# A searched list schedule against a written fixed order per engine: two attention and two feed-forward layers on one core

## The chip, the cores and the metric

One core of one Trainium2 chip. The metric is the device time of one execution in microseconds (us), the median over several executions. Each execution also has a mean granted TensorE clock, as a share of full speed.

## The reference, cut to what matters

Two pairs of layers with the same weights, on x of 2048 x 512: linear attention with 32 heads of 16, then a ReGLU feed-forward of 1376 columns.

```python
def _A_ref(x, wqkv, w_phi, wo):
    ...
    phi_k = concatenate([softmax(pk), softmax(-pk)], -1)      # phi_q likewise
    kv  = einsum("bhsf,bhsd->bhfd", phi_k, v)                 # over ALL 2048 rows
    z   = einsum("bhsf->bhf", phi_k)
    num = einsum("bhqf,bhfd->bhqd", phi_q, kv)
    den = einsum("bhqf,bhf->bhq", phi_q, z)[..., None] + 1e-6
    return (num / den).transpose(...).reshape(B, S, D) @ wo
def _B_ref(x, W_gate, W_up, W_down):
    gate = relu(x @ W_gate); return (gate * (x @ W_up)) @ W_down
x = A_x
x = x + _A_ref(_layernorm(x), ...);  x = x + _B_ref(_layernorm(x), ...)
x = x + _A_ref(_layernorm(x), ...);  x = x + _B_ref(_layernorm(x), ...)
```

`kv` is a sum over all rows, so no row's numerator can start before the last row's K and V are done. Each attention layer thus holds a serial passage, and the feed-forward layers are long stretches of independent matmuls.

## The kernel before: the parts that matter

The kernel lists 3748 operations, each with its engine, its reads and writes, a duration and a name. Dependencies follow from reads and writes. A list scheduler then decides which operation stands where on each engine; 20 seeded perturbations, found by a search, are applied in a row.

```python
WINDOW = {"sp": 24, "act": 64, "pe": 400, "dve": 40, "pool": 24}

    def schedule(self):
        self.setup_search()
        best = self.first_order()          # list scheduling, forward and backward passes
        for seed in self.STEPS:            # 20 seeded perturbations of the priorities
            best = self.step(best, seed)
        _, start, finish, _ = best
        ...
        self.order = sorted(self.ops, key=lambda o: (o.start, o.idx))
        return self.order
```

From the order, `prepare` plans the fewest semaphore waits; each engine runs its list in sequence. Three groups of operations are named in the argument below:

```python
    def knorm(self, t, tag):               # K normalisation, one tile of 128 rows
        op("dve", ... tensor_reduce ..., f"{tag} Zk {t}")
        op("dve", ... reciprocal ..., f"{tag} rZk {t}")
        parts = [("pool", 0, 2)] if t < NT - 2 else [("pool", 0, 1), ("dve", 1, 2)]
        ...                                # GpSimd: expk *= 1/Zk           "phik"
    def kv_acc(self, t, tag):              # 8 matmuls of 65 columns        "kvacc"
        ...  [r("phik", t, bank), r("v", t), r("vones")], [self.RP[bank]] ...   # banks 0 and 1
    def q_proj(self, st, ring, tag, ...):  # groups of 4 matmuls of 512     "q st c"
        ...  banks = [next(ring) for _ in range(w)] ...
    def num(self, t, nring, wring, tag):   # 8 matmuls of 144 columns       "num"
        ...  [r("expq", st, c, s), r("kvbd", s, 0), r("kvbd", s, 1), ...] ...
```

Between the last "kvacc" and the first "num", VectorE writes the accumulated sums as block matrices ("kvbd"). The "q" groups have no part in that and can stand there as filler.

The softmax here doesn't subtract the row's maximum and nothing guards it: scores larger than these inputs give would overflow.

Of the kernel before, what the change touches and what calls it, by code (L numbers as in the profile page):

```python
# [10 lines left out]
ALL_STREAMS = ENG_NAMES + DMA_QUEUES  # L11

# [38 lines left out]
class Program:  # L51
# [9 lines left out]
    WEIGHTS = (5.0, 10.0, 20.0, 30.0)  # L61
    PASSES = 12
    STEPS = (
        540311766, 892937877, 494555537, 744661157, 897750461, 867948165, 881829396, 760774381, 571941922, 293543564,
        578814794, 296541888, 687658138, 1028335485, 543616021, 388973925, 782538568, 34231468, 301009185, 271859956,
    )

    def __init__(self, nc, window, n_dma_sems=48):
        self.nc = nc
        self.ops = []  # L70
        self.window = window
        self.n_dma_sems = n_dma_sems
# [54 lines left out]
    def setup_search(self):  # L127
        self._derive_deps()
        ops = self.ops
        n = len(ops)  # L130
        self.succ = [[] for _ in range(n)]
        for o in ops:
            for d in o.deps:
                self.succ[d].append((o.idx, True))
            for d in o.order_deps:
                self.succ[d].append((o.idx, False))
        rank = [0.0] * n
        for o in reversed(ops):
            lat = o.lat if o.lat is not None else self.DMA_START + o.dma_bytes / self.DMA_BW + self.DMA_TAIL
            rank[o.idx] = max([rank[q] + (lat + self.TO[ops[q].eng] if d else o.occ) for q, d in self.succ[o.idx]], default=lat)  # L140
        self.rank = rank

    def first_order(self):
        best = None
        for weight in self.WEIGHTS:
            prio = [weight * o.idx - self.rank[o.idx] - o.boost for o in self.ops]
            for _ in range(self.PASSES):
                span, start, finish = self._forward(prio)
                if best is None or span < best[0]:
                    best = (span, start, finish, prio)  # L150
                prio = [t - o.boost for t, o in zip(self._backward(start, finish), self.ops)]
        return best

    def step(self, best, seed):
        ops = self.ops
        span, start, finish, prio = best
        rng = random.Random(seed)
        kind = seed % 4
        a = rng.uniform(0.0, span)
        w = (6e3, 15e3, 40e3, span)[int(rng.random() * 4)]  # L160
        amp = (150.0, 500.0, 1500.0, 4000.0)[int(rng.random() * 4)]
        share = (0.02, 0.1, 0.4, 1.0)[int(rng.random() * 4)]
        base = prio if kind < 2 else [s - o.boost for s, o in zip(start, ops)] if kind == 2 else [t - o.boost for t, o in zip(self._backward(start, finish), ops)]
        new = []
        for o in ops:
            x, y = rng.random(), rng.random()
            p = base[o.idx]
            if a - w / 2 <= start[o.idx] <= a + w / 2 and x < share:
                p += (2 * y - 1) * amp
            new.append(p)  # L170
        span, start, finish = self._forward(new)
        return span, start, finish, new

    def schedule(self):
        self.setup_search()
        best = self.first_order()
        for seed in self.STEPS:
            best = self.step(best, seed)
        _, start, finish, _ = best
        self.makespan = max(finish)  # L180
        for o in self.ops:
            o.start, o.finish = start[o.idx], finish[o.idx]
        self.order = sorted(self.ops, key=lambda o: (o.start, o.idx))
        return self.order

    def _forward(self, prio):
        ops, succ, TO = self.ops, self.succ, self.TO
        n = len(ops)
        npred = [len(o.deps) + len(o.order_deps) for o in ops]
        ready = [0.0] * n  # L190
        avail = {e: {} for e in ENG_NAMES}
        pending = {e: [o.idx for o in ops if o.eng == e] for e in ENG_NAMES}
        place = [0] * n
        for e in ENG_NAMES:
            for j, i in enumerate(pending[e]):
                place[i] = j
        done = [False] * n
        free = {e: 0.0 for e in ENG_NAMES}
        q_free = 0.0
        pool_end = dve_end = 0.0  # L200
        first = {e: 0 for e in ENG_NAMES}
        for o in ops:
            if npred[o.idx] == 0:
                avail[o.eng][o.idx] = 0.0
        start, finish = [0.0] * n, [0.0] * n
        nxt = {e: None for e in ENG_NAMES}
        dirty = set(ENG_NAMES)
        inf = float("inf")
        for _ in range(n):
            for e in dirty:  # L210
                lst = pending[e]
                f = first[e]
                while f < len(lst) and done[lst[f]]:
                    f += 1
                first[e] = f
                lim = f + self.window[e]
                fe = free[e]
                if e == "pool":
                    fe = max(fe, dve_end - self.PORT_POOL)
                bt, bp, bi = inf, inf, -1  # L220
                for i, t in avail[e].items():
                    if place[i] >= lim:
                        continue
                    if t < fe:
                        t = fe
                    if e == "dve":
                        pt = ops[i].port
                        if pt is not None and t < pool_end - pt:
                            t = pool_end - pt
                    if t < bt or (t == bt and (prio[i] < bp or (prio[i] == bp and i < bi))):  # L230
                        bt, bp, bi = t, prio[i], i
                nxt[e] = (bt, bp, bi) if bi >= 0 else None
            dirty = set()
            st, _, i = min(k for k in nxt.values() if k is not None)
            o = ops[i]
            e = o.eng
            start[i] = st
            free[e] = st + o.occ
            if o.lat is None:
                q_free = max(st + self.DMA_START, q_free) + o.dma_bytes / self.DMA_BW  # L240
                fin = q_free + self.DMA_TAIL
            else:
                fin = st + o.lat
            finish[i] = fin
            if e == "pool":
                pool_end = fin
                dirty.add("dve")
            elif e == "dve" and o.port is not None:
                dve_end = fin
                dirty.add("pool")  # L250
            done[i] = True
            del avail[e][i]
            dirty.add(e)
            for q, is_data in succ[i]:
                eq = ops[q].eng
                npred[q] -= 1
                if is_data:
                    t = fin + TO[eq]
                    if t > ready[q]:
                        ready[q] = t  # L260
                if npred[q] == 0:
                    avail[eq][q] = ready[q]
                    dirty.add(eq)
        return max(finish), start, finish

    def _backward(self, start, finish):
        ops, succ, TO = self.ops, self.succ, self.TO
        n = len(ops)
        T = max(finish)
        nsucc = [len(x) for x in succ]  # L270
        late = [T] * n
        avail = {e: set() for e in ENG_NAMES}
        free = {e: T for e in ENG_NAMES}
        for o in ops:
            if nsucc[o.idx] == 0:
                avail[o.eng].add(o.idx)
        out = [0.0] * n
        nxt = {e: None for e in ENG_NAMES}
        dirty = set(ENG_NAMES)
        for _ in range(n):  # L280
            for e in dirty:
                nxt[e] = min([(-min(late[i] - (finish[i] - start[i]) + ops[i].occ, free[e]), -finish[i], i) for i in avail[e]], default=None)
            dirty = set()
            k, _, i = min(x for x in nxt.values() if x is not None)
            o = ops[i]
            out[i] = free[o.eng] = -k - o.occ
            avail[o.eng].remove(i)
            dirty.add(o.eng)
            for d in o.deps + o.order_deps:
                e = ops[d].eng  # L290
                nsucc[d] -= 1
                late[d] = min(late[d], out[i] - TO[o.eng] if d in o.dset else out[i] + (finish[d] - start[d]) - ops[d].occ)
                if nsucc[d] == 0:
                    avail[e].add(d)
                    dirty.add(e)
# [735 lines left out]
```

## Time and profile before

| | before |
|---|---|
| median of 4 runs beside the changed kernel | 394.75 us (393.81 to 395.34) |
| profiled span, mean clock | 391.6 us, 0.999 |
| TensorE work at its full rate | 363.1 us |
| first matmul starts | 3.21 us |
| last K/V accumulation of layer 0 | 54.18 us |
| first numerator matmul of layer 0 | 56.76 us |
| last K/V accumulation of layer 2 | 238.99 us |
| last matmul starts | 388.25 us |

The third row is the sum over all 2379 matmuls of the start-to-start time of each shape, as the prediction works it out. In the trace of this kernel, neighbouring matmuls of one shape start 216 ns apart at 512 columns (median; between 82 and 236 us also where two groups alternate), 109 at 256, 82 at 192, 63 at 144 and 32 at 65; at 128 columns it is mostly 107 in the first 12 us and 56 from 18.9 us on. The times below it are starts of matmuls, found by laying the trace beside the program's order. Together they give a measure, called the **loss** of a stretch: time between the first and the last start in it, less the full-rate work of the matmuls that start there. The lines of the profile itself are shown in the prediction.

### The profile page before, as it was taken

What the parts mean: (1) busy time and instruction counts of PE and PEld (TensorE: products, weight loads), DVE (VectorE), ACT (ScalarE), POOL (GpSimd) and SP (SyncE); (2) the same over time, 40 slices, a digit from 0 to 9 for tenths busy, and PEclk for the clock granted to TensorE, in tenths of its full rate; (3) what the DMA queues carried; (4) which work ended last, traced back from release to release, by engine and by line L of the source; (5) the groups of instructions that cost most, each with busy time, mean ns of one, the idle gap of its engine ahead of it and who ended that gap; (6) DMA issues with size and microseconds to landing.
All of it is one profiled execution on the core that took longest, in us unless ns stands there. A gap on an engine that the chain in (4) does not pass through costs nothing.

```text
span 391.6 us, 6419 instructions
## 1 busy us (share of the span) xinstructions
PE 369.0 (94%) x2336; PEld 201.8 (52%) x2379; DVE 268.1 (68%) x551; ACT 201.5 (51%) x381; POOL 170.2 (43%) x287
## 2 busy tenths in 40 slices
PE   5898988999999999999999997979999999999996
PEld 4444444576744554454444464456774445454443
DVE  5989878887766889766675776978875676322222
ACT  5787869742643413534354475965652561443340
POOL 7597952771543383533433652466544252000000
PEclk9999999999999999999999999999999999999999
DMA  6752492332221225301110120233233123100001
GB/s 195 195 80 57 114 364 53 70 65 47 54 51 29 41 54 83 68 2 27 27 15 0 27 28 2 41 62 68 62 69 79 27 43 83 41 13 15 27 28 55
DMA packets 66080, 24.08 MB, mean 61 GB/s; under 512 B 57888, under 2 KB 65024, under 8 KB 66048
## 3 DMA queue, kind: packets, MB, share of 16 engines
q1 hardware_dynamic: 65328, 23.07, 26.3%
q10 hardware_dynamic: 720, 0.59, 0.5%
q8 instruction: 19, 0.31, 0.4%
q14 instruction: 13, 0.11, 0.1%
HBM read 7.91 MB, written 2.10 MB: 26 GB/s over the span
## 4 chain that ended last, share of the span: by engine, by line
PE 84%; DMA 5%; DVE 4%; ACT 3%; issue 2%; POOL 1%; SPq 0%; POOLq 0%; DVEq 0%
PE ps L795 34%; PE ps L844 19%; PE ps L654 9%; PE ps L774 6%; PE ps L727 5%; PE ps L685 3%; PE ps L743 3%; PE ps L821 2%; DMA oT<-osb 2%; PE ps L699 2%; DMA yT<-ytile 1%; ACT expq L730 1%; DMA x_sb<-in_A_x_dram 1%; DVE tsc L763 1%; ACT expk L688 0%
## 5 line engine op out<-in xcount | busy, mean ns | idle before, releaser
L795 PE MATMUL ps<-yT,Wgu 128*128 128x512 bf16 (+1 forms) x789 | 173.8, 336 | 0.5
L795 PEld LDWEIGHTS ps<-yT,Wgu 128*128 128x128 bf16 x800 | 75.7, 98 | 62.0 <-ACT expk L803 1.4
L844 PE MATMUL ps<-Wd,hT 128*128 128x512 bf16 (+2 forms) x356 | 103.5, 373 | 0.4
L797 ACT ACTIVATE gate_sb<-ps 128x512 bf16<-128x512 f32 (+1 forms) x100 | 50.4, 513 | 82.7 <-PE ps L795 71.8
L673 POOL TENSOR_TENSOR expk<-expk,rZk 128x1024 bf16<-128x1024 bf16 (+1 forms) x32 | 59.6, 1876 | 33.1 <-DVE rZk L668 27.6
L844 PEld LDWEIGHTS ps<-Wd,hT 128*128 128x128 bf16 (+1 forms) x363 | 35.2, 98 | 35.8
L805 DVE TENSOR_TENSOR hT<-gate_sb,expk 128x512 bf16<-128x512 bf16 (+1 forms) x65 | 26.8, 422 | 29.4 <-ACT expk L803 23.4
L588 DVE BATCH_NORM_STATS2 stats<-x_sb 128x6 f32<-128x512 bf16 x64 | 42.6, 680 | 4.8 <-DMA x_sb<-in_A_x_dram 4.2
L401 ACT ACTIVATE numbf<-ps 128x432 bf16<-128x432 f32 x64 | 33.0, 539 | 20.1 <-PE ps L743 19.5
L666 DVE TENSOR_REDUCE Zk<-expk 128x64 f32<-128x1024 bf16 x32 | 38.1, 1205 | 4.5 <-ACT expk L688 2.6
L846 DVE TENSOR_TENSOR x_sb<-x_sb,ps 128x512 bf16<-128x512 bf16 (+1 forms) x33 | 22.0, 670 | 26.8 <-PE ps L844 26.6
L768 POOL TENSOR_TENSOR osb<-tsc 128x512 bf16<-128x512 bf16 x28 | 32.3, 1155 | 17.6 <-DVE tsc L763 17.6
L774 PE MATMUL ps<-wo_p,oT 128*128 128x512 bf16 x117 | 35.3, 379 | 3.9 <-DMA oT<-osb 3.5
L727 PE MATMUL ps<-yT,Wqp 128*128 128x512 bf16 x123 | 34.6, 379 | 2.3 <-ACT expq L730 2.1
L730 ACT ACTIVATE expq<-ps 128x1024 bf16<-128x1024 f32 (+1 forms) x40 | 32.2, 861 | 7.2 <-PE ps L727 5.9
L743 PE MATMUL ps<-kvbd,expq 128*128 128x144 bf16 x256 | 33.6, 226 | 2.4 <-DVE kvbd L716 2.1
L595 POOL TENSOR_SCALAR rv<-mv 128x1 f32<-128x1 f32 (+1 forms) x53 | 12.6, 240 | 53.6 <-DVE mv L590 53.1
L803 ACT ACTIVATE expk<-ps 128x512 bf16<-128x512 f32 (+1 forms) x65 | 32.2, 501 | 6.3 <-PE ps L795 6.2
L596 POOL TENSOR_TENSOR rstd<-rv,mhalf 128x1 f32<-128x1 f32 (+1 forms) x53 | 31.5, 597 | 3.0
L631 DVE TENSOR_SCALAR ytile<-x_sb,mv,rstd 128x512 bf16<-128x512 bf16 x52 | 22.1, 426 | 12.4 <-POOL rstd L596 11.7
L754 POOL TENSOR_TENSOR zm<-numbf 128x64 f32<-128x64 bf16 x28 | 10.5, 375 | 45.8 <-DVE numbf L401 33.0
L657 ACT ACTIVATE expk<-ps 128x512 bf16<-128x512 f32 x44 | 23.7, 603 | 12.5 <-PE ps L654 12.0
(78 smaller groups left out, 428.9 us busy)
## 6 DMA issues: line engine op xcount, KB each, us to landing
out_dram<-x_sb SPq DMA_DIRECT2D x15, 128.0 KB, 1.7
x_sb<-in_A_x_dram SPq DMA_DIRECT2D x3, 512.0 KB, 6.4
Wgu<-in_B_W_gate_dram SPq DMA_DIRECT2D x4, 344.0 KB, 4.0
Wgu<-in_B_W_up_dram SPq DMA_DIRECT2D x4, 344.0 KB, 5.9
Wd<-in_B_W_down_dram SPq DMA_DIRECT2D x5, 256.0 KB, 7.7
yT<-ytile SPq DMA_TRANSPOSE x60, 2.5
hT<-in_A_wqkv_dram ACTq DMA_DIRECT2D x4, 128.0 KB, 3.0
x_sb<-in_A_x_dram SPq DMA_DIRECT2D x4, 128.0 KB, 3.5
```

The source lines that it names most:

```text
L401: return e.activation(out, in_, ACT.Copy) if hasattr(e, "activation") else e.tensor_copy(out, in_)
L588: op("dve", (lambda t: lambda e: e.bn_stats(k.stats6[:, t, :], k.x_sb[:, t, :]))(t), [r("x", t)], [r("st", t)], 685, f"{tag} stats {t}")
L654: op("pe", (lambda ic, bank, W: lambda e: e.matmul(k.pb[bank][:], k.yT[:, ic, t * 128:(t + 1) * 128], W[:, ic, :], start=(ic == 0), stop=( ...
L666: op("dve", lambda e: e.tensor_reduce(k.Zk[:, zb, :], k.expk[:, t, :, :, :].rearrange("p g s (h f) -> p (g s h) f", f=16), AX.X, ALU.add), ...
L673: op(eng, (lambda kv, u0, n: lambda e: e.tensor_tensor(kv, kv, k.rZk[:, rb, u0 * 32:u0 * 32 + n].unsqueeze(2).to_broadcast([P, n, 16]), AL ...
L727: op("pe", (lambda c, ic, bank: lambda e: e.matmul(k.pb[bank][:], k.Wqp[:, ic, c * 128:(c + 1) * 128], k.yT[:, ic, st * 512:(st + 1) * 512 ...
L730: op("act", (lambda c0, s, b0: lambda e: e.activation(k.expq[:, st, c0:c0 + w, s, :], k.ps[:, b0:b0 + w, :], ACT.Exp, scale=(1.0 - 2.0 * s ...
L743: op("pe", (lambda s, c, j, g0, bank: lambda e: e.matmul(k.pb[bank][:, j * GW:(j + 1) * GW], k.expq[:, st, c, s, tt * 128:(tt + 1) * 128], ...
L774: op("pe", (lambda c, bank: lambda e: e.matmul(k.pb[bank][:], k.oT[:, ob, c, :], k.wo_p[:, c, :], start=(c == 0), stop=(c == NC - 1)))(c, ...
L795: op("pe", (lambda bank, W, ic, fc, Mf: lambda e: e.matmul(k.pb[bank][0:Mf, 0:n], W[:, ic, fc * 128:fc * 128 + Mf], k.yT[:, ic, c0:c0 + n] ...
L797: op("act", (lambda Mf, gb, gs: lambda e: e.activation(k.gate_sb[0:Mf, gs, 0:n], k.pb[gb][0:Mf, 0:n], ACT.Relu))(Mf, gb, gs), [self.RP[gb] ...
L844: op("pe", (lambda fc, Kf, u, c0, bank, m0, m1: lambda e: e.matmul(k.pb[bank][:, m0:m1], k.hT[0:Kf, u, c0:c0 + 128], k.Wd[0:Kf, fc, m0:m1] ...
```

## The change

The scheduler goes. A written table gives, for each engine, the sequence of operation numbers in base 36; `schedule` only simulates that order to get start times for planning the waits. The order is said to have been annealed (improved by random moves) against an in-order simulation with drawn DMA delays and noise on durations; the code doesn't show how it was found. Matmuls of one accumulation group nearly always stay together. The operations and their dependencies are the same.

```diff
+ORDER = {
+    "act": ("6 7 9 8 15 1a 10 24 1p 1k 2o 1u 2e 3t 3u 2y 3d 3v 4h 4f 4g 3j 5l 5n 5m 68 69 ..."),
+    "dve": ("1v 1w v 25 26 1z 2f 2g 29 2p 1f 2q 2j 33 35 2z 31 30 34 32 36 2t 4u 4t 4w 4v ..."),
+    "pool": ("p 2 n 0 3 1 4 j 1x 1y q 27 28 m 2h 2i 2r 2s 37 38 3c k 39 l 3f o 3i 4x 4y 4z ..."),
+    "pe": ("r s t u 11 12 13 14 w x y z 16 17 18 19 1b 1c 1d 1e 20 21 22 23 1l 1m 1n 1o ..."),
+    "sp": ("a 5 b c d e g f h i 3e 3b 3h 3k 56 58 5c 5a 8p 8n 8t 8r 9a 9f 8v 8x 97 94 8z ..."),
+}
...
     def schedule(self):
-        self.setup_search()
-        best = self.first_order()
-        for seed in self.STEPS:
-            best = self.step(best, seed)
-        ...
+        self._derive_deps()
+        seq = {e: [int(x, 36) for x in ORDER[e].split()] for e in ENG_NAMES}
+        assert sorted(i for s in seq.values() for i in s) == list(range(len(ops)))
+        ...                       # start times by stepping through seq in order
         return self.order
-    def _forward(self, prio): ...
-    def _backward(self, start, finish): ...
```

(Tables and functions are cut.) As a static check I wrote the old order as such a table: the program that comes out is the old one, waits included. So the order is all that differs.

## The prediction

> **What bounds the kernel now.** I read the page's busy rows first, then a table of engine time by stretch, then the waits, then the timelines of TensorE, GpSimd and VectorE where the table shows holes.
>
> ```profile
> span 391.6 us, 6419 instructions
> PE 369.0 (94%) x2336; PEld 201.8 (52%) x2379; DVE 268.1 (68%) x551; ACT 201.5 (51%) x381; POOL 170.2 (43%) x287
> ```
>
> TensorE is the bound: 94% busy, nobody else above 68%. There are 2379 weight loads, one for each matmul, but 2336 matmul rows, so 43 matmul records are missing and small "gaps" of a whole matmul are not gaps. The same by stretch (columns: stretch, then busy time and count for PE, weight loads, DVE, ACT, POOL, then clock, DMA share, GB/s):
>
> ```profile
> 0.00:13.00 13.00, 7.75 (x52) 5.38 (x54) 7.83 (x21) 7.49 (x13) 7.35 (x25) 1.00 0.73 233
> 13.00:57.00 44.00, 39.30 (x296) 20.20 (x300) 39.49 (x59) 35.04 (x52) 36.37 (x38) 1.00 0.55 140
> 57.00:82.00 25.00, 22.79 (x172) 13.98 (x172) 20.59 (x53) 19.60 (x36) 12.76 (x28) 1.00 0.37 86
> 82.00:236.00 154.00, 152.64 (x914) 81.18 (x932) 112.91 (x221) 65.14 (x131) 70.32 (x108) 1.00 0.21 37
> 236.00:262.00 26.00, 20.72 (x169) 11.95 (x169) 18.60 (x47) 19.40 (x29) 10.02 (x20) 1.00 0.20 37
> 262.00:388.00 126.00, 125.25 (x741) 68.94 (x753) 67.85 (x154) 54.79 (x122) 33.37 (x70) 1.00 0.20 47
> ```
>
> Idle TensorE time is stretch minus busy: 5.3 in the opening, 4.7 in the first K/V stage, 2.2 where the first attention goes over into the feed-forward part, 1.4 in 154 us of full work, 5.3 at the second such passage, 0.8 in the next 126 us, and 3.6 after 388 (last residual and store). So two passages and the opening hold nearly all of it; 280 us of the span are full, and no order can shorten them. What TensorE waits for (total, times, longest):
>
> ```profile
> PE ps L774 <- DMA oT<-osb: 3.5, 3, 2.7
> PE ps L546 <- DMA hT<-in_A_wqkv_dram: 3.2, 1, 3.2
> PE ps L685 <- DMA yT<-ytile: 2.2, 2, 1.3
> PE ps L727 <- ACT expq L730: 2.1, 2, 1.1
> PE ps L743 <- DVE kvbd L716: 2.1, 2, 1.6
> ```
>
> The 3.2 is the first load and stays. The others are links of two serial chains: K normalisation up to the accumulated K·V, and from there num, normalise, transpose by DMA, output projection, layer norm, transpose by DMA, first gate matmul. In the K/V stage GpSimd is a second bound (timeline of POOL):
>
> ```profile
> 14.37 0.23 POOL L595 TENSOR_SCALAR rv<-mv 128x4 f32<-128x4 f32 x1 [4.39 <-DVE mv L590]
> 33.99 3.86 POOL L673 TENSOR_TENSOR expk<-expk,rZk 128x1024 bf16<-128x1024 bf16 x2 [0.76 <-DVE rZk L668]
> 39.70 14.32 POOL L673 TENSOR_TENSOR expk<-expk,rZk 128x1024 bf16<-128x1024 bf16 x8 [1.84 <-DVE ytile L629]
> ```
>
> From 14.37 to 39.70 + 14.32 = 54.0 it works all but 0.76 + 1.84 = 2.6 us, and the first layer's last accumulation can only follow it.
>
> [...]from 147.84 us on, 24 recorded gate/up matmuls of 512 columns take 5.56 us; less the last one's 0.379 that is 5.18 between first and last start, 225 ns over 23 steps, or 216 over 24, as one record is missing there. That gives the floor: 1333 matmuls of 512 columns x 0.2157 + 342 of 256 x 0.109 + 128 of 192 x 0.0825 + 256 of 144 x 0.0625 + 256 of 65 x 0.032 + 64 of 128 x 0.056 = 363 us (shapes from the groups by form, counts completed from the program). The span stands 391.6 - 363 = 28.6 above it. [...]201.8 us of weight loads lie beside 152.64 busy in 154. So interleaving two groups, as the old order does, costs TensorE nothing by itself, and running groups whole saves nothing by itself.
>
> **The change part by part.** The instruction order tool shows the same 3748 operations with the same dependencies; only the order on each engine, and the waits that follow from it, differ. Nothing is removed or added, so busy times per engine stay (369, 268, 201, 170), and the gain must come out of 28.6 us. Of these, 3.2 (first load), 3.6 (tail: both orders end on the last tile's 22 half-width down matmuls, then residual and store) and about 2 (the first 48 narrow matmuls run at some 0.1 us apart against 0.057 later) are fixed. About 20 us can be moved.
>
> On TensorE, runs of equal instructions fall from 887 to 346: groups of 4 (11 for down) stay together. A group that shared TensorE with another finishes up to 4 x 0.2157 = 0.86 us earlier when it runs alone, so its evacuation starts earlier, while the second ends when it did. In the full stretches that is slack; on the chains it is worth something.
>
> *First passage, to 82 us.* Before, VectorE puts the first K reduction (1.18) ahead of the last layer-norm aggregate, so GpSimd starts its block at 14.37. After, the aggregates of tiles 4 to 7 come first: about 1.4 earlier (1.18 and the 0.2 of an aggregate that stood behind it). GpSimd then finishes the statistics of tiles 8 to 11 before its first two K products (3.82 together) and not after; their normalised rows, transposes and K matmuls come up to 4 us earlier, which should remove most of the 2.2 us wait for yT and part of the 2.6 us idle on GpSimd. Its work is fixed at 39.65 - 2.6 = 37 us, so it ends at best near 14.37 - 1.4 + 37 = 50, against 54.0; I take half of the idle as removed: 54.0 - 1.4 - 1.3 = 51.3, so 2.7. The new order has then done 6 query matmuls (1.3 us) less, which serve as filler in the chain behind. There the old order lost 2.2 and the new one puts output projections 0 and 1 right behind each other some 7 us after the first num, where the old one needed 64.68 - 56.76 = 7.9: some wait stays. Net 0.5. Together 3.2.
>
> *Second passage, 236 to 262.* Rows of the TensorE timeline:
>
> ```profile
> 241.01 0.42 PE L743 MATMUL ps<-kvbd,expq 128*128 128x144 bf16 x4 [1.61 <-DVE kvbd L716]
> 241.89 0.30 PE L743 MATMUL ps<-kvbd,expq 128*128 128x144 bf16 x2 [0.45 <-DVE kvbd L716]
> 250.76 1.04 PE L774 MATMUL ps<-wo_p,oT 128*128 128x512 bf16 x4 [0.43 <-DMA oT<-osb]
> 259.94 0.81 PE L774 MATMUL ps<-wo_p,oT 128*128 128x512 bf16 x3 [2.68 <-DMA oT<-osb]
> ```
>
> The new order leaves one query group (0.86) between the last accumulation and num where the old one left one matmul (0.2): 2.1 falls to about 1.4. Output projection 0 then stands 5 x 0.86 + 28 x 0.0625 = 6.1 after the first num; the chain needs about 7.3 (old 249.15 - 241.01 = 8.1, less 0.6 as num now runs whole, rounded for waits), so 1.2 is lost. Projection 3 has a first gate group and more queries ahead of it: of its 2.68 I keep 0.3, and 0.9 for the transposed rows of tile 1. Sum 3.8 against 5.8 idle in the old order with the small ones: 2.0 gained.
>
> *Full stretches.* 2.2 us of idle together. A fixed order tried against drawn delays may save some and whole groups may lose some: 0.3 gained. *Tail:* 0.
>
> Sum 3.2 + 2.0 + 0.3 = 5.5, so 395.0 - 5.5 = **389.5**.
>
> **The rivals.** *The order does what it was made for:* an annealed order takes most of the movable 20 us, say 9: 386. For it: it was judged under delays, and the old one was a greedy list with 20 perturbations. Against it: GpSimd's 37 us of work and the two DMA transposes of 2.4 us in each passage are serial whatever the order. *New waits take their place:* with coarser groups TensorE has fewer points at which to slip filler in; one late transpose (the longest landing was 4.5 us against 2.4) stops everything behind it. 154 us at 99% busy would drop to 98%: +1.5 there and +1 in the other full stretch, gains in the passages as above or half: 390 to 395. *The chains decide and nothing moves:* the passages are bound by VectorE and ScalarE (18.6 and 19.4 busy of 26): 393 to 395. Three weight loads (344, 344 and 256 KB) now stand between output transposes 1 and 2 on the same queue; at 343 GB/s, the rate of the stretch from 50 to 60 us, their 0.94 MB cost 2.8 us if a transpose gets behind them.
>
> **Range and chances.** 5.5 is a sum of two passages each unsure by some 2 us, and full stretches by 1.5: about 3.2 together, 4 at 80%, wider on the fast side for the first rival. Range 384.5 to 394. Faster by 2% means under 387.2, 2.3 below my middle: 0.27. Slower by 2% needs 8 us of new waits in a kernel that is full for 280 us: 0.04. Within 2%: 0.69.
>
> **What would show it.** Right: busy sums unchanged; idle TensorE in the first 82 us from 12.2 to about 9, at the second passage from 5.3 to about 3.5, elsewhere within 1 us of 2.2; GpSimd's last K product of the first layer near 51; the longest wait for oT below 1.5. Wrong: idle over 4 us in the full stretches (second rival), GpSimd's block ending at 54 again (third), or both passages under half of their idle time (first). A wait for weights of the feed-forward part would be a miss of mine altogether.

## The result, and the profile after

The changed kernel takes **389.93 us** (median of 4 runs, 388.86 to 391.21) against 394.75 us (4 runs, 393.81 to 395.34): ratio **0.988**, 95% interval 0.984 to 0.992. A ratio is the mean time of one kernel's fast runs over that of the other's of the same rounds, so not quite the ratio of the medians quoted.

The head of the page of the changed kernel, to be laid beside the first lines of the prediction:

```profile
span 389.5 us, 6419 instructions
PE 373.7 (96%) x2379; PEld 203.0 (52%) x2379; DVE 264.8 (68%) x551; ACT 202.3 (52%) x381; POOL 168.5 (43%) x287
```

The busy time of TensorE rose from 369.0 to 373.7 while the kernel got shorter. Its work has not grown: this trace has all 2379 matmul records, the one before lacked 43, and this one holds a stretch at half clock (below). Of the 4.7 us some 2.9 are the missing records, as rows laid into the holes give, and 1.7 the half clock. By stretch (columns: stretch; busy time and count of PE, weight loads, DVE, ACT, POOL; clock, DMA share, GB/s):

```profile
0.00:13.00 13.00, 7.22 (x51) 4.92 (x52) 8.28 (x23) 6.15 (x11) 7.70 (x24) 1.00 0.70 219
13.00:57.00 44.00, 41.16 (x313) 21.04 (x312) 39.02 (x62) 37.55 (x57) 35.88 (x40) 0.98 0.54 137
57.00:82.00 25.00, 24.05 (x176) 15.13 (x175) 19.24 (x48) 19.23 (x35) 12.92 (x29) 0.97 0.37 92
82.00:236.00 154.00, 154.00 (x942) 81.05 (x941) 114.81 (x222) 64.67 (x130) 70.30 (x108) 1.00 0.20 38
236.00:262.00 26.00, 23.66 (x181) 13.81 (x180) 19.70 (x51) 21.15 (x36) 11.55 (x25) 1.00 0.20 40
262.00:388.00 126.00, 123.64 (x727) 67.02 (x724) 63.80 (x151) 53.57 (x115) 30.20 (x64) 1.00 0.20 47
```

The second row has 313 matmuls and the fourth 942, against 296 and 914 before. Part of that is only the missing records; the weight loads, of which none is missing, rise by 12 and 9, so more work does get done in the same time. What TensorE waits for (total, times, longest):

```profile
PE ps L511 <- DMA hT<-in_A_wqkv_dram: 3.9, 1, 3.9
PE ps L708 <- DVE kvbd L681: 3.7, 4, 1.4
PE ps L708 <- ACT numbf L366: 1.5, 3, 0.6
```

Of the five waits that the prediction shows, the ones for oT (3.5 us) and for yT (2.2 us) are gone from the top. The wait for kvbd has grown, and copies of the numerator (numbf) are new. GpSimd in the first K/V stage:

```profile
12.50 0.30 POOL L560 TENSOR_SCALAR rv<-mv 128x4 f32<-128x4 f32 x1 [2.11 <-DVE mv L555]
...
30.17 18.20 POOL L638 TENSOR_TENSOR expk<-expk,rZk 128x1024 bf16<-128x1024 bf16 x10
49.52 1.50 POOL L638 TENSOR_TENSOR expk<-expk,rZk 128x512 bf16<-128x512 bf16 x1 [1.15 <-ACT expq L695]
```

Its block starts at 12.50 instead of 14.37 and ends at 49.52 + 1.50 = 51.02 instead of 54.0. TensorE just behind it:

```profile
53.12 0.42 PE L708 MATMUL ps<-kvbd,expq 128*128 128x144 bf16 x4 [1.39 <-DVE kvbd L681]
54.45 0.42 PE L708 MATMUL ps<-kvbd,expq 128*128 128x144 bf16 x4 [0.91 <-DVE kvbd L681]
54.72 1.67 PE L692 MATMUL ps<-yT,Wqp 128*128 128x512 bf16 x4
56.18 0.69 PE L708 MATMUL ps<-kvbd,expq 128*128 128x144 bf16 x4
56.66 1.88 PE L692 MATMUL ps<-yT,Wqp 128*128 128x512 bf16 x4
58.36 0.42 PE L708 MATMUL ps<-kvbd,expq 128*128 128x144 bf16 x4
...
239.38 0.42 PE L708 MATMUL ps<-kvbd,expq 128*128 128x144 bf16 x4 [0.97 <-DVE kvbd L681]
240.26 0.42 PE L708 MATMUL ps<-kvbd,expq 128*128 128x144 bf16 x4 [0.45 <-DVE kvbd L681]
```

Look at the four query matmuls from 56.66 to 58.36: 1.70 us, or 425 ns each, where 216 is the full rate. The same stretch in steps of 2 us says it in the clock column, the third from the end:

```profile
54.00:56.00 2.00, 1.54 (x8) 0.78 (x9) 1.27 (x6) 1.26 (x3) 0.00 (x0) 0.74 0.09 31
56.00:58.00 2.00, 2.00 (x9) 0.99 (x8) 1.23 (x3) 0.77 (x2) 0.00 (x0) 0.50 0.00 0
58.00:60.00 2.00, 2.00 (x16) 1.08 (x14) 1.00 (x4) 1.30 (x2) 0.00 (x0) 0.91 0.00 0
```

After two waits of 1.39 and 0.91 us with 0.42 us of work between them, TensorE ran at half clock for some 3.4 us, from 54.95 to 58.37. A row of "PE 2.00 busy" hides it; the count (x9 in place of x16) gives it away.

Ahead of the last matmul the 13 kept traces hold eight half-clock stretches, in seven traces; the trace of the kernel before has none (its clock record begins at 12.0 us). In the rerun of the changed kernel one follows the same two waits (1.38 and 0.91 us; four query matmuls from 56.20 to the next start at 57.91, 428 ns each). In the run e1_first_part_new (below) the same two waits of 1.39 and 0.91 us stand at the same place, and the clock stayed full there: four query matmuls from 54.91 to 55.77, 215 ns each. So in two of these traces the waits go before half clock and in one they don't; what decides it isn't shown.

Losses of the two kernels, stretch by stretch. "after" is the profiled execution of the rerun of the changed kernel, which also has the half-clock stretch:

| stretch | loss before | loss after | difference |
|---|---|---|---|
| before the first matmul | 3.21 | 3.82 | +0.6 |
| first matmul to last accumulation of layer 0 | 10.56 | 7.25 | -3.3 |
| from there to the first numerator | 1.25 | 1.55 | +0.3 |
| from there to the end of the first 1200 operations | 3.71 | 4.74, or 3.36 without the half clock | -0.35 |
| full stretch, to the last accumulation of layer 2 | 0.28 | 0.48 | +0.2 |
| from there to the first numerator of layer 2 | 1.78 | 1.14 | -0.6 |
| from there to the down matmuls of tile 8 | 4.26 | 3.37 | -0.9 |
| the rest | 0.15 | 0.17 | 0 |

The 3.36 is from the run e1_first_part_new, which has the same order in that stretch and whose clock was not cut there. Without the half clock the differences sum to -4.1 us; untraced executions at full clock differ by 4.9 to 5.2 (below), so about a microsecond of the gain is not placed by these two traces. The last row but one holds two opposite changes: in the first 21 us behind the first numerator the loss falls from 4.0 to 2.5, and in the long stretch after that it rises from 0.3 to 0.9.

### The profile page after: what moved, and what is told of

Its sections match the earlier page's. It is cut to its first block, busy times and chain, and to the rows that moved or that the text cites.

```text
span 389.5 us, 6419 instructions
## 1 busy us (share of the span) xinstructions
PE 373.7 (96%) x2379; PEld 203.0 (52%) x2379; DVE 264.8 (68%) x551; ACT 202.3 (52%) x381; POOL 168.5 (43%) x287
## 4 chain that ended last, share of the span: by engine, by line
PE 88%; DMA 5%; ACT 2%; DVE 2%; POOL 1%; SPq 0%; issue 0%; ACTq 0%
PE ps L760 34%; PE ps L809 20%; PE ps L619 10%; PE ps L692 7%; PE ps L739 6%; PE ps L708 4%; PE ps L650 3%; PE ps L786 2%; PE ps L664 2%; DMA wv_p<-in_A_wqkv_dram 2%; DMA yT<-ytile 1%; DMA hT<-in_A_wqkv_dram 1%; DMA hT<-h10t 1%; DVE kvbd L676 1%; ACT numbf L366 1%; ACT expk L653 1%
## 5 line engine op out<-in xcount | busy, mean ns | idle before, releaser
L760 PE MATMUL ps<-yT,Wgu 128*128 128x512 bf16 (+1 forms) x800 | 153.0, 336 | 0.5 <-DVE h10t L791 0.5
L809 PE MATMUL ps<-Wd,hT 128*128 128x512 bf16 (+2 forms) x363 | 80.3, 373 | 0.0
L366 ACT ACTIVATE numbf<-ps 128x432 bf16<-128x432 f32 x64 | 33.9, 533 | 22.4 <-PE ps L708 20.8
L770 DVE TENSOR_TENSOR hT<-gate_sb,expk 128x512 bf16<-128x512 bf16 (+1 forms) x65 | 23.8, 381 | 26.9 <-ACT gate_sb L762 16.7
L695 ACT ACTIVATE expq<-ps 128x1024 bf16<-128x1024 f32 (+1 forms) x40 | 33.3, 865 | 8.9 <-PE ps L692 7.2
L560 POOL TENSOR_SCALAR rv<-mv 128x1 f32<-128x1 f32 (+1 forms) x53 | 13.1, 250 | 51.8 <-DVE mv L555 51.7
L596 DVE TENSOR_SCALAR ytile<-x_sb,mv,rstd 128x512 bf16<-128x512 bf16 x52 | 23.4, 460 | 14.2 <-POOL rstd L561 11.8
L739 PE MATMUL ps<-wo_p,oT 128*128 128x512 bf16 x128 | 32.5, 379 | 0.0
L708 PE MATMUL ps<-kvbd,expq 128*128 128x144 bf16 x256 | 27.4, 228 | 5.2 <-DVE kvbd L681 3.7
L561 POOL TENSOR_TENSOR rstd<-rv,mhalf 128x1 f32<-128x1 f32 (+1 forms) x53 | 30.5, 580 | 3.2
```

Source lines behind the costliest of these rows:

```text
L366: return e.activation(out, in_, ACT.Copy) if hasattr(e, "activation") else e.tensor_copy(out, in_)
L695: op("act", (lambda c0, s, b0: lambda e: e.activation(k.expq[:, st, c0:c0 + w, s, :], k.ps[:, b0:b0 + w, :], ACT.Exp, scale=(1.0 - 2.0 * s ...
L708: op("pe", (lambda s, c, j, g0, bank: lambda e: e.matmul(k.pb[bank][:, j * GW:(j + 1) * GW], k.expq[:, st, c, s, tt * 128:(tt + 1) * 128], ...
L739: op("pe", (lambda c, bank: lambda e: e.matmul(k.pb[bank][:], k.oT[:, ob, c, :], k.wo_p[:, c, :], start=(c == 0), stop=(c == NC - 1)))(c, ...
L760: op("pe", (lambda bank, W, ic, fc, Mf: lambda e: e.matmul(k.pb[bank][0:Mf, 0:n], W[:, ic, fc * 128:fc * 128 + Mf], k.yT[:, ic, c0:c0 + n] ...
L809: op("pe", (lambda fc, Kf, u, c0, bank, m0, m1: lambda e: e.matmul(k.pb[bank][:, m0:m1], k.hT[0:Kf, u, c0:c0 + 128], k.Wd[0:Kf, fc, m0:m1] ...
```

## The experiments

All kernels compute the right result. "At full clock" means the mean over the executions whose granted clock was 0.998 or more. With the old order these took 393.65 us (6 executions, 393.05 to 394.41) beside the first four experiments, 393.57 us (7) beside the next four, and 393.39 us (4) beside the last three. These three batches ran on three different chips, and the changed kernel itself ran only in the first; its 388.46 below is the mean of two runs, 388.76 with the two at full clock of the first measurement. At full clock the runs of one kernel still spread by up to 3 us (391.28 to 394.25 for one of them), so differences of well under a microsecond between such means aren't told apart.

### The changed kernel again

No edit.

> The changed kernel once more, unedited, with more runs. In its profile TensorE's granted clock fell to half for some 3 us at 55 us, right behind two waits of 1.6 and 1.1 us before and inside the first num group; the two runs with a mean clock of 0.995 took 391.2 and 390.6, the two with 1.000 took 389.2 and 388.9. Theory (a clock drop that comes in some runs): the runs fall in two groups about 1.9 us apart, told by the mean clock. Rival (drop is there in all runs, the spread is other noise): one group, no relation to the clock.

Measured: 390.31 us (388.33 to 391.37, 6 runs) against 394.41 (11 runs), ratio 0.988 (0.985 to 0.992). The runs fall in two groups: 388.59 and 388.33 at clock 1.000; 390.62, 391.37, 390.0 and 390.8 at 0.996. The old order has both groups as well: mean 393.65 at 1.000, and 395.16 (5 runs) at 0.995 to 0.996. Like against like, the gain is 393.65 - 388.46 = 5.2 us at full clock and 395.16 - 390.70 = 4.5 us below it. So the loss of clock is no effect of the change alone; it costs 1.5 us in one kernel and 2.2 in the other.

### The first part of the new order alone

```diff
+P = set(the first 1200 operations of the old order by start time)
+order[e] = [i for i in new[e] if i in P] + [i for i in old[e] if i not in P]
```

> The first 1200 operations (up to about 107 us, the first passage) in the new relative order, all behind them in the old one. By the prediction's terms the first passage brings 3.2 and the rest 2.3: this kernel should be 3.2 faster than before, less whatever the half clock at 55 us takes (1.9): 391.5 to 393.4. Rival (the gain is all in the second passage and the full stretches): within 1 us of before, 394 to 395.

Measured: 393.05 us (390.6 to 394.12), ratio 0.996 (0.992 to 0.999). Four of six runs were below full clock; the two at 0.999 took 391.07 and 390.6, so 2.8 us less than the old order. The first 1200 operations ended 2.55 us earlier (102.70 against 105.25), which fits. The loss of the full stretch behind rose from 0.28 to 1.30: about a microsecond is the price of the seam between two orders that weren't made for each other.

### The rest of the new order alone

```diff
+order[e] = [i for i in old[e] if i in P] + [i for i in new[e] if i not in P]
```

Here P is the first 1200 operations by the start times of the new order; it differs from the P above in four operations.

> The converse: the first 1200 operations in the old order, the rest in the new one. By the prediction's terms 2.3 faster than before (2.0 second passage, 0.3 full stretches): 392.4. From the trace of the changed kernel I would now say 3.0 to 3.5 (idle 5.9 to 3.7 in the second passage, 1.9 to 1.6 in the rest): 391.5. Rival (the new order pays only as a whole): under 1 us. The two gains of this and the run before should add up to that of the whole change.

Measured: 393.15 us (391.28 to 394.25), ratio 0.997 (0.994 to 0.999), all six runs at full clock, mean 393.04: only 0.6 us less than the old order. Too little for what was expected, though with six runs that spread by 3 us. The loss from the first numerator of layer 2 on was 4.31, not the 3.37 of the whole new order, and that of the full stretch 0.75, not 0.48. The parts alone save 2.8 + 0.6 = 3.4 us, together some 5. The seam of the first part's run, 0.8 to 1.0, is part of the difference. Of the 1.2 here only 0.3 lie just behind the seam; 0.6 are a wait for a transposed tile at 322 us, far behind it, and the remaining 0.3 are within the spread of the traces. That seams make up the whole difference isn't shown.

### Whole groups in the old order

TensorE's groups put together at the place of their last member, all else in the old order. This asks whether the property named in the change, whole groups, is what pays.

```diff
+last = {group of i: its last position in old["pe"]}
+order["pe"] = sorted(old["pe"], key=lambda i: (last[group(i)], position of i))
```

> The old order with one thing changed: the matmuls of each group stand together, at the place where the group's last one stood; all other engines keep the old order. Theory of the prediction (running groups whole saves nothing by itself where TensorE is full, something on the chains): 0 to 1 us faster. Rival (the whole groups are what pays): 3 us or more faster. Other rival (fewer places for filler): 1 to 3 us slower.

Measured: **399.52 us** (397.55 to 400.69), ratio 1.013 (1.010 to 1.016): slower, and the expectation was wrong. At clock 1.000 there is one run, 397.55, so +3.9 us. The first waits of TensorE in this run:

```profile
PE ps L708 <- DVE kvbd L681: 3.7, 3, 2.3
PE ps L708 <- ACT numbf L366: 3.2, 8, 0.9
...
PE ps L739 <- DMA oT<-osb: 2.1, 1, 2.1
```

The last accumulation came 1.6 us earlier (52.56 against 54.18), but behind it the filler stood in the wrong places: 2.3 us before the first numerator in one piece, and eight waits for numerator copies. The profiled execution lost clock as well (0.990). So whole groups alone, put where their last member stood, cost; another place wasn't tried. That the annealed order pays because the other engines' sequences and the fillers were fitted to its groups is argued from this, not shown.

### More work for GpSimd in the first K/V stage

In the new order, a fill of 1.06 us on GpSimd behind the K products of tile 3; its target is a buffer that is written anew before anyone reads it.

```diff
+        op("pool", lambda e: e.memset(k.numbf[:, 0, :, :], 0.0), [], [r("numbf", 0, gb) for gb in range(3)], 1060, "pad")
```

> The new order with one useless memset of 1.06 us on GpSimd in the first K/V stage, behind its product of tile 3 (its block there runs from 12.5 to 51.0 with 1.4 us idle). The time at equal mean clock is compared with the new order's 388.5 at clock 1.000 and 390.7 at 0.996. Theory of the prediction (GpSimd's block sets the end of the first K/V stage): 0.7 to 1.1 us slower, and first num 0.7 to 1.1 later. Rival (TensorE's own work or ScalarE sets it by now): 0 to 0.3.

The start of GpSimd's block in the rerun of the changed kernel, then the block with the fill:

```profile
12.31 0.30 POOL L560 TENSOR_SCALAR rv<-mv 128x4 f32<-128x4 f32 x1 [2.02 <-DVE mv L555]
```

```profile
13.31 0.30 POOL L561 TENSOR_SCALAR rv<-mv 128x4 f32<-128x4 f32 x1 [2.87 <-DVE mv L556]
...
28.65 1.06 POOL L501 MEMSET numbf<- 128x1152 bf16 x1
29.67 1.93 POOL L639 TENSOR_TENSOR expk<-expk,rZk 128x1024 bf16<-128x1024 bf16 x1
31.56 0.20 POOL L580 TENSOR_TENSOR nmr<-agg,rstd 128x4 f32<-128x4 f32 x1
31.71 20.11 POOL L639 TENSOR_TENSOR expk<-expk,rZk 128x1024 bf16<-128x1024 bf16 x11
```

Measured: 391.19 us (390.22 to 392.25), ratio 0.992 (0.989 to 0.996). At full clock the three runs took 390.40 against 388.46 of the changed kernel; at 0.996 three runs took 392.05 against 390.70. So a microsecond on GpSimd costs 1.3 to 1.9 (with the two runs of the first measurement 1.6 instead of 1.9). In the trace, against the rerun of the changed kernel, the last accumulation moved by 1.19 us (52.66 against 51.47), the first numerator by 1.18, the first gate matmul by 1.19 and layer 2's last accumulation by 1.21. But that pair of traces proves little by itself: in this execution the block had already started 1.0 us later (13.31 against 12.31), as VectorE waited 0.76 us for rows of x, and of the two delays, 1.00 + 1.06, only 0.91 was left at the block's end, as the pauses that it has in the rerun (0.35 and 1.15) took up the rest. What carries the conclusion is the untraced times, longer in both clock groups, while the old order beside them took the same as before: in the new order too, GpSimd's block sets the end of the first K/V stage. How much of one microsecond reaches the end is known only roughly.

### A filler in front of the first numerator

In the new order, query group "q 1 2" behind the last accumulation, where the 1.39 us wait is.

```diff
-"pe": ... q 1 2 (4) ... kvacc 15 (8) | num 0 (4) | num 0 (4) | q ...
+"pe": ...               kvacc 15 (8) | q 1 2 (4) | num 0 (4) | num 0 (4) | q ...
```

> The new order with one query group of the first layer moved from ahead of the last K.V accumulations to right behind them, so that TensorE has 0.86 us of work where it idled for 1.6 ahead of the first num. Theory[...]: the mean clock is 1.000 in most runs and the median falls to 388.5 or a little under. Rival (the clock drops for another reason, a run's own phase): still about half of the runs at 0.996, median 390.

```profile
51.76 0.42 PE L708 MATMUL ps<-kvbd,expq 128*128 128x144 bf16 x4 [0.54 <-DVE kvbd L681]
53.10 0.42 PE L708 MATMUL ps<-kvbd,expq 128*128 128x144 bf16 x4 [0.91 <-DVE kvbd L681]
```

Measured: 389.07 us (388.35 to 390.64), ratio 0.988 (0.985 to 0.991). All six runs were at clock 0.998 or more, where the changed kernel had four of ten there. The wait fell from 1.39 to 0.54 and the half-clock stretch is absent from this trace (span 386.6 against 388.9). But the mean at full clock, 389.22, is not below the changed kernel's 388.46 (388.76 over four runs); the ratios to the old order are the same within the interval. The two waits left here are 0.54 and 0.91; whether the shorter one is what kept the clock full in these six runs isn't shown. The filler moves a wait; whether it gains anything at full clock isn't shown.

### An earlier load of the small weights

In the new order, the load of w_phi ahead of the first rows of x, as a test of the 0.6 us by which the first matmul starts later.

```diff
-"sp": x0, ..., phi, ...
+"sp": phi, x0, ...
```

> The new order with the first two loads of the queue swapped back as in the old order (the small phi ahead of x tile 0). In the new order's profiles TensorE's first matmul is 0.6 later than in the old one (3.8 against 3.2) and its second step waits 0.8 for GpSimd's product with phi. Theory (the opening's idle time is beside the GpSimd block that sets the K/V stage's end): under 0.4 us of gain at equal clock, perhaps none as x tile 0 comes 0.5 later. Rival (the opening counts in full): 1 us faster or more.

Measured: 390.66 us (388.62 to 390.88), ratio 0.990 (0.987 to 0.993). The first matmul started at 3.20 instead of 3.82, but the last accumulation at 51.27 against 51.47, and the last matmul of all at 385.44 against 385.56. The later start is off the path: GpSimd's block didn't start sooner (12.77, against 12.50 and 12.31 in the two traces of the changed kernel). Two runs at clock 1.000 took 388.6 and 388.8 and two 390.6 and 390.8, so the clock column doesn't account for all of the two groups.

### VectorE and GpSimd in the new order, in the K/V stage only

Old order, with the new sequence of these two engines for all that stands ahead of the first numerator.

```diff
+for e in ("dve", "pool"): order[e] = new order of old[e]'s K/V-stage operations + the rest of old[e]
```

> The old order on TensorE, ScalarE and the DMA queue, with VectorE's and GpSimd's operations of the first K/V stage alone put in the new relative order (layer-norm aggregates ahead of the first K reduction, statistics of tiles 8 to 11 finished ahead of the first K products). The prediction laid most of the first passage's 2.7 to this. Theory: first num 1.5 to 3 us earlier than 56.8, time 1.5 to 3 us under the old order's at equal clock (393.6 at 1.000, 395.2 at 0.996). Rival (it takes the other engines' order as well): under 1 us.

Measured: 395.69 us (394.11 to 398.09), ratio 1.006 (1.002 to 1.009). No gain; the theory fell. GpSimd's block did start earlier, at 12.75, but had idle in it again (1.30 us early, 0.91 and 0.82 in the later part) and ended at 53.3: its inputs come from TensorE and ScalarE, which still stood in the old order. Five of six runs were below full clock, so the half per cent itself means little.

### All engines but TensorE, and all engines, in the K/V stage only

The same edit for VectorE, GpSimd, ScalarE and the DMA queue; and for these and TensorE.

```diff
+for e in ("dve", "pool", "act", "sp"):        ...   # e10
+for e in ("dve", "pool", "act", "sp", "pe"):  ...   # e11
```

> Old order, and the new order of VectorE, ScalarE, GpSimd and the DMA queue over the first layer's K/V stage; TensorE in the old order throughout. What it asks: what did the run with VectorE and GpSimd alone lack, the other side engines or TensorE? Theory: the block of K products on GpSimd (32.5 us of work) waits for inputs that TensorE makes in the old sequence, so it again starts its last products with idle ahead of them, ends at 53 to 54 us, and the time at full clock is 393 to 395.5 us. Rival: ScalarE's old order was what held it up; then the accumulations end near 51.5 us and the time is 390.5 to 391.5.

> Old order, and the new order of all five sequences over the first layer's K/V stage alone (everything that stands ahead of the first layer's numerator); the rest as before. Theory: GpSimd's block runs from 12.5 us almost without a pause, the last accumulation falls at 51.3 to 51.8 us, 2.4 to 2.9 us before the kernel before, and what follows keeps most of it: at full clock 391 to 392 us. Rival: the gain of the first passage needs the new order behind the numerator as well; then the old order gives the lead back by the first gate matmul and the time is 393 to 394.

Measured without TensorE: **402.09 us** (400.19 to 406.08), ratio 1.022 (1.018 to 1.026). Far worse than either expectation. Measured with TensorE: **390.44 us** (389.83 to 392.38), ratio 0.992 (0.989 to 0.994); the five runs at full clock took 390.26 against 393.39, so 3.1 us less. GpSimd with the old TensorE sequence:

```profile
35.81 1.93 POOL L638 TENSOR_TENSOR expk<-expk,rZk 128x1024 bf16<-128x1024 bf16 x1 [2.16 <-DVE rZk L633]
...
41.30 5.76 POOL L638 TENSOR_TENSOR expk<-expk,rZk 128x1024 bf16<-128x1024 bf16 x3 [3.57 <-DVE rZk L633]
47.81 8.61 POOL L638 TENSOR_TENSOR expk<-expk,rZk 128x1024 bf16<-128x1024 bf16 x5 [0.75 <-DVE rZk L633]
```

and with the new one:

```profile
30.36 18.18 POOL L638 TENSOR_TENSOR expk<-expk,rZk 128x1024 bf16<-128x1024 bf16 x10
49.69 1.50 POOL L638 TENSOR_TENSOR expk<-expk,rZk 128x512 bf16<-128x512 bf16 x1 [1.15 <-ACT expq L695]
```

Ten products without a pause, and the last accumulation at 51.67 us instead of 54.18; in the mixed run it was at 61.79. Each engine runs its list in order, so a sequence on one engine was only as good here as the sequences that fed it. This one stage gives 3.1 of the some 5 us. The rest of the old order keeps its lead: the first 1200 operations end 2.3 us earlier, layer 2's last accumulation 2.3.

### Fillers in both attention layers

The version that might have beaten both: as the filler above, and in layer 2 the group "q 1 1" ahead of the first numerator.

```diff
-"pe": ... q 1 3 (4) |             num 0 (4) | num 0 (4) | q 1 1 (4) | num 1 ...
+"pe": ... q 1 3 (4) | q 1 1 (4) | num 0 (4) | num 0 (4) |             num 1 ...
```

> The new order with the group of query matmuls behind the last accumulation in the first layer, as in the run that tried that, and in the second layer too: the group q 1 1 ahead of the first numerator group. Theory: the second layer's wait for the cleared block matrices (0.97 us) is covered by the group's 0.86 us, and the numerator groups behind it are then ready at once, so the end comes 0.4 to 0.9 us earlier than with the first filler alone: 388.2 to 388.7 us at full clock, with the first layer's half-clock stretch absent in all or nearly all runs. Rival: the group is missed where it stood, between the numerator groups, whose wait for ScalarE's copies (0.6 us) grows by as much; then 388.9 to 389.4 and no gain.

```profile
235.10 1.02 PE L692 MATMUL ps<-yT,Wqp 128*128 128x512 bf16 x4
237.97 1.04 PE L692 MATMUL ps<-yT,Wqp 128*128 128x512 bf16 x4 [1.84 <-DVE kvbd L681]
```

Measured: 390.55 us (389.22 to 391.86), ratio 0.991 (0.988 to 0.994); at full clock 389.9. No gain, and the trace says why: the filler itself waited 1.84 us for kvbd. Its PSUM bank is one of the two that held the accumulation, so it depends on the same VectorE reads as the numerator. Moving a filler ahead of a wait helps only if the filler's buffer isn't freed by that same wait; the list of dependencies would have told me. Two of the six runs were below full clock, so the first filler doesn't keep every execution there either; the traced execution kept its clock (1.000), so where those two lost it isn't shown.

## Why the prediction was right

The predicted 389.5 us met 389.9; as a gain, 5.5 us were predicted (from 395.0) and 4.8 measured. The signs it named came true: TensorE's idle time fell from 12.2 to 9.6 us in the first 82 us (predicted about 9), from 5.3 to 2.3 at the second passage (about 3.5), elsewhere it went from 2.2 to 2.4, and none of TensorE's listed waits is for oT any more (predicted: the longest below 1.5). That the sum comes so close is partly luck, as its terms err in both directions. Step by step:

- **First K/V stage, predicted 2.7 us earlier: right.** The last accumulation came at 51.5 to 51.7 us against 54.18, so 2.5 to 2.7. GpSimd's block ended at 51.02; predicted was 51.3. The two terms in it were uneven: it started 1.9 us earlier (predicted 1.4), and the idle left in it is about 1.4 (0.28 and 1.15; predicted 1.3). The times with the fill on GpSimd show that this block sets the stage's end, and the run with all engines in this stage alone gets 3.1 us. The cause that the prediction named, VectorE's and GpSimd's own new sequence, carries only the earlier start (12.75 in the run that changed these two alone); there 3.0 us of idle came in behind it, so the second term needs the other engines' order, which the prediction didn't say.
- **Behind it, net 0.5 more: not seen.** The first part alone ended its 1200 operations 2.55 us earlier, about what the accumulation had gained (2.4). So the whole first passage gave 2.5 to 2.8, not 3.2: the loss ahead of the first numerator grew from 1.25 to 1.55, and the one behind it fell by as little, from 3.71 to 3.36. The waits for oT that went were replaced by waits for kvbd (1.39 and 0.91).
- **Second passage, predicted 2.0: right in kind and about in size.** The wait for kvbd was 0.97 + 0.45 = 1.4, as predicted; the loss ahead of the first numerator fell from 1.78 to 1.14, the same in every trace of either order. In the 21 us behind it the old order loses 3.4 to 4.0 in the three traces in which the clock wasn't cut there, the new one 2.5 to 2.9 in the six that have the new order and no added filler there. So the passage gains between 1.1 and 2.1. The waits for oT vanished altogether, where I had left 1.2 + 0.3 + 0.9 for them and for transposed rows; waits for the numerator's copies, which I hadn't named, came instead (0.6 and 0.3 in the rerun's trace). The working has a slip: 8.1 - 0.6 is 7.5 and not 7.3, and the 5.8 us that it starts from are 5.3 in its own table.
- **Full stretches, predicted 0.3 gained: wrong in sign.** The loss of the first went from 0.28 to 0.48, and that of the second from some 0.3 to between 0.8 and 1.0 in five traces of the new order; most of the latter is one new wait near 291 us, for the last columns' products (PE <- DVE h10t, 0.4 in the rerun's trace). The prediction read 1.4 us of idle in the first out of the busy rows. Most of it is holes that missing records leave: a recorded matmul of 512 columns lasts 0.38 us and two starts of full-rate work lie 0.43 us apart, so each hole shows as some 0.05 us or more, and 18 records are missing in this stretch. With a row of the usual length laid into each hole, 0.2 of the 1.4 us remain. The prediction said that such holes are no gaps and then counted them.
- **Tail 0: right.** From the last matmul's start to the end it was 3.3 us before and 3.3 to 3.6 after.
- **The clock: not in the prediction.** About half of the executions of either order have a mean clock below full and take on average 0.9 to 2.2 us longer; in the trace of the changed kernel it is one stretch at half clock. The gain is 5.2 us among runs at full clock (4.9 over all four) and 4.5 among the others.

The rivals: *new waits take their place* was right that new waits come (kvbd 3.7 us against 2.1, numerator copies 1.5), but these some 3 us are less than the waits that went (oT 3.5, yT 2.2, expq 2.1). *The order takes most of the movable 20 us* is refuted: the losses behind the first matmul still are 18.7 of 22.0 us in the traced executions (17.3 without the half clock). *Nothing moves* is refuted by GpSimd's end at 51.02.

Shown by runs: GpSimd's block as the limit of the first stage; that its gain needs all engines; that whole groups alone cost. Shown by traces alone: that waits of 1.39 and 0.91 us go before half clock in some executions, and the gain of the second passage, as the run with the rest of the new order alone shows only 0.6 us. Only argued: that the seam accounts for the whole difference between the parts and the sum. Open: what sets off half clock; why the filler's lower wait doesn't show at full clock, and why two groups of times appear even at clock 1.000 (in the runs with w_phi first and with both fillers); loads that land later in some executions, as in the trace with the fill, are one candidate.

## What to carry to other kernels

Before valuing a new order, find the one engine that works through the serial stage nearly without a pause, here GpSimd with 37 us of work in its block (12.50 to 51.02 less 1.4); for that stage an order is worth about what it starts that engine's block earlier and what idle it takes out of it. Orders of engines belong together: a better sequence on some of them, without those that feed it, made this kernel 2% slower (402.09 us against 393.81), and one seam between two orders cost about a microsecond. Measure idle time by start-to-start losses, not by busy rows, and before moving a filler ahead of a wait check which buffer it writes.
